# The last keys' products of an attention step put between its whole-chunk scores and its whole-chunk attn @ v

## The chip, the cores and the metric

The kernel runs on one core of one Trainium2 chip. The metric is the device time of one execution in microseconds. A core has TensorE (matmuls, PE in the profile; its loads of weights are PEld), VectorE (DVE), ScalarE (ACT), GpSimd (POOL) and SyncE (SP, which here only issues DMAs). Matmuls write to PSUM, and VectorE and ScalarE read it from there.

## What is computed

```python
def _attn_ref(q, k, v):                      # each (8, 12, 448, 64): batch, heads, sequence, width of a head
    scale = 1.0 / np.sqrt(q.shape[-1])
    scores = scale * np.matmul(q, k.transpose(0, 1, 3, 2)) - np.log(S)
    attn = 1.0 / (1.0 + np.exp(-scores))     # sigmoid, no softmax
    return np.matmul(attn, v)

def reference(q, k, v, w_in, w_out, s, b):
    x = attn_out.transpose(0, 2, 1, 3).reshape(B * S, H * D)   # 3584 x 768
    h = np.maximum(x @ w_in, 0.0)            # 3584 x 2048
    return (s * (h * h) + b) @ w_out         # 3584 x 768
```

## The kernel before

Attention comes first, in 24 steps (n = 0 to 23), and the feed-forward part fills the rest of the time. A step takes one batch and a quad of four heads: two pairs i = 0, 1, each with two heads j on the halves of the 128 partitions. The scores are computed with keys on the partitions. The 448 keys of a head are three whole chunks of 128 keys (c = 0, 1, 2) and 64 last keys. So a step has six tiles of whole-chunk scores (i, c), each for two heads, and one tile for the last keys of all four heads.

TensorE does four things in a step, each with its own shape of matmul. A shape such as 64\*128 in the profile says how many rows and columns of the array one matmul takes.

- `scores` (line 413, 64\*128): the six whole-chunk tiles. From step 1 on each is made of three products, since q and k are split into a high and a low part (qkh, qkl); 36 matmuls. Step 0 has single products of unsplit data (line 419).
- `attn_v` (line 445, 128\*64): the six tiles of sigmoids times v, 24 matmuls (12 pairs) that add up in the PSUM tile pav.
- `scores_last` (line 434, 64\*64): the last keys' scores, psc_l, 8 matmuls in two groups of four, for step n + 1. Step 0 does its own as well.
- `attn_v_last` (line 454, 64\*64): the last keys' sigmoids times v, 8 matmuls in two groups of four that also add into pav.

ScalarE turns each tile of scores into a tile of sigmoids (`sigmoid`, line 394), in the order (0,0), (0,1), (0,2), (1,0), (1,1), (1,2); then it makes the high part of the next step's q and k, does some jobs on weights (line 208, 258 and others), and takes the last-keys sigmoid a_l for the next step. VectorE makes the low part, converts weights, and copies pav out (`store_x`, line 461).

The order on each engine is that of the code, since the schedule is manual. PSUM is what ties the engines to each other. The pool ps_qk has three buffers with the tag psc, which are taken in turn:

```python
pl, tag = (ps_av, "pav") if (i, c) == (0, 2) else (ps_qk, "psc")
o = psc[i, c] = pl.tile([P, 2, 512], F32, tag=tag, name=f"psc_{b}_{t}_{i}_{c}")
...
psc = ps_qk.tile([P, 2, 512], F32, tag="psc", name=f"psc_{b}_{t}_l")
```

So chunk (0, 2) is computed in the one buffer of ps_av, which then becomes pav, and the other five and the last keys' tile go through the three buffers of ps_qk. From step 1 on TensorE takes them in the order (0,0), (0,1), (1,0), (0,2), (1,1), (1,2). A tile that takes a used buffer waits until the sigmoid that read the old one has ended.

Of the kernel before, what the change touches and what calls it, by code (L numbers as in the profile page):

```python
# [11 lines left out]
F32 = mybir.dt.float32  # L12
# [82 lines left out]
def sigmoid_attention_relu2_ffn(  # L95
# [11 lines left out]
    B, NQ, P, _, _, S = qk.shape  # L107
    D = v.shape[5]
    NF, _, DM = w_in.shape
# [13 lines left out]
    def pool(stack, name, bufs, side=None, space=None):  # L123
        kw = dict(side=side) if side else {}
        if space is not None:
            kw["space"] = space
        return stack.enter_context(
            tc.tile_pool(name=name, bufs=bufs, reuse_waits="tile", **kw)
        )
# [22 lines left out]
    first = ExitStack()  # L152
# [201 lines left out]
    ps_av = pool(at, "ps_av", 1, space=PSUM, side="right")  # L354
# [5 lines left out]
    def load(b, t, first=False):  # L360
        x = ld.tile([P, 2, 2, S], F32, tag="qk", name=f"qk_{b}_{t}")
        if first:
            nc.sync.dma_start(x[:, 0, 1, :P], qk[b, t][:, 0, 1, :P])
            nc.scalar.dma_start(x[:, 0, 0], qk[b, t][:, 0, 0])
            nc.sync.dma_start(x[:, 0, 1, P:], qk[b, t][:, 0, 1, P:])
            nc.scalar.dma_start(x[:, 1, 0], qk[b, t][:, 1, 0])
            nc.sync.dma_start(x[:, 1, 1], qk[b, t][:, 1, 1])
        else:
            nc.sync.dma_start(x, qk[b, t])
        return [x]  # L370

    def load_v(b, t, ld_):
        vt = ldv.tile([P, 7, 2, D], F32, tag="v", name=f"v_{b}_{t}")
        nc.sync.dma_start(vt, v[b, t])
        ld_.append(vt)
# [6 lines left out]
    def parts_hi(b, t, ld_):  # L382

        hi, lo = (hl.tile([P, 2, NX], F32R, tag=h, name=f"qk{h}_{b}_{t}") for h in "hl")
        nc.scalar.copy(hi, flat(ld_[0]))
        ld_.append((hi, lo))

    def parts_lo(ld_):
        hi, lo = ld_[-1]
        sub(lo, flat(ld_[0]), f32(hi))  # L390
# [6 lines left out]
    def scores(b, t, ld_):  # L397
        x = ld_[0]
        two = ld_.pop() if len(ld_) > 2 else None
        a = {}  # L400
        psc = {}
        order = [(i, c) for i in range(2) for c in range(3)]
        if two:
            order[2:4] = order[3], order[2]
        for i, c in order:

            pl, tag = (ps_av, "pav") if (i, c) == (0, 2) else (ps_qk, "psc")
            o = psc[i, c] = pl.tile([P, 2, 512], F32, tag=tag, name=f"psc_{b}_{t}_{i}_{c}")
            if two:
                cols = slice(S + c * P, S + (c + 1) * P)  # L410
                for m, (wi, xi) in enumerate(PARTS):
                    for j, r in enumerate(half):
                        nc.tensor.matmul(  # L413
                            o[:, j, :S], two[wi][r, i, cols], two[xi][r, i, :S],
                            start=m == 0, stop=m == 2,
                        )
            else:
                for j, r in enumerate(half):
                    nc.tensor.matmul(  # L419
                        o[:, j, :S], x[r, i, 1, c * P : (c + 1) * P], x[r, i, 0, :],  # L420
                        start=True, stop=True,
                    )
            if two and i + c == 1 and i:
                continue
            for k in [(i, c)] + [(1, 0)] * (two is not None and (i, c) == (0, 2)):
                a[k] = sigmoid(psc[k], f"{b}_{t}_{k[0]}_{k[1]}")
        return a

    def scores_last(b, t, ld_):
        x = ld_[0]  # L430
        psc = ps_qk.tile([P, 2, 512], F32, tag="psc", name=f"psc_{b}_{t}_l")
        for j, r in enumerate(half):
            for i in range(2):
                nc.tensor.matmul(  # L434
                    psc[half[i], j, :S], x[r, i, 1, 3 * P :], x[r, i, 0, :],
                    start=True, stop=True,
                )
        return sigmoid(psc, f"{b}_{t}_l")

    def attn_v(b, t, ld_, a):  # L440
        pav = ps_av.tile([P, 2, 512], F32, tag="pav", name=f"pav_{b}_{t}")
        for i in range(2):
            for c in range(3):
                for j, r in enumerate(half):
                    nc.tensor.matmul(  # L445
                        pav[r, i, :S], ld_[1][:, 3 * i + c, j, :], a[i, c][:, j, :],
                        start=c == 0, stop=False,
                    )
        return pav

    def attn_v_last(ld_, a, pav):
        for i in range(2):
            for j, r in enumerate(half):
                nc.tensor.matmul(  # L454
                    pav[r, i, :S], ld_[1][half[i], 6, j, :], a[half[i], j, :],
                    start=False, stop=True,
                )

    def store_x(b, t, pav):
        o = xo.tile([P, 2, S], F32, tag="xo", name=f"xo_{b}_{t}")  # L460
        nc.vector.tensor_copy(o, pav[:, :, :S])
        nc.sync.dma_start(x_dram[b][:, 2 * t : 2 * t + 2], o)

    loaded = {0: load(*quads[0], first=True)}
# [18 lines left out]
    def ticks(n, part):  # L483
        for _, _, fn in sorted(plan.pop((n, part), ()), key=lambda x: x[:2]):
            fn()
# [98 lines left out]
    for n, (b, t) in enumerate(quads):  # L584
        ticks(n, "DVE")
        a = scores(b, t, loaded[n])
        if n == 0:
            al = scores_last(b, t, loaded[0])
        if n + 1 in TWO:
            parts_hi(*quads[n + 1], loaded[n + 1])  # L590
        ticks(n, "ACT")
        if n + 2 < NL:
            loaded[n + 2] = load(*quads[n + 2])
        ticks(n, "SP")
        for fn in stores:
            fn()
        stores.clear()
        if n == NL - 1:
            qkx.close()
            ps_h = pool(blk_ps, "ps_h", 2, space=PSUM)  # L600
        pav = attn_v(b, t, loaded[n], a)
        last = al
        if n + 1 < NL:
            al = scores_last(*quads[n + 1], loaded[n + 1])
        attn_v_last(loaded[n], last, pav)
        if n + 1 in TWO:
            parts_lo(loaded[n + 1])
        ticks(n, "END")
        store_x(b, t, pav)
        if n + 2 < NL:  # L610
            load_v(*quads[n + 2], loaded[n + 2])
# [142 lines left out]
    start = [(0, 0), (2, 0), (2, 1), (2, 2), (0, 2), (0, 1), (1, 1), (1, 2), (1, 0)]  # L754
# [175 lines left out]
    for n, blocks in enumerate(threes):  # L930
# [128 lines left out]
        for u, (i, p) in enumerate(L1):  # L1059
# [10 lines left out]
            for j in range(2):  # L1070
                m = 0
                for c in range(KC):
                    for wi, xi in PARTS:
                        nc.tensor.matmul(  # L1074
                            bk[:, j], wt[:, j, wi, c * P : (c + 1) * P], opd[i][xi][:, c, :],
                            start=i == ch[0] and m == 0,
                            stop=m == 3 * KC - 1,
# [111 lines left out]
        for j, (i, p) in enumerate(L2):  # L1189
# [8 lines left out]
            for e, tk in LAST if end else [(e, slice(TB)) for e in range(KC)]:  # L1198
# [3 lines left out]
                for f in range(2):  # L1202
                    for m, (wi, gi) in enumerate(PARTS):
                        nc.tensor.matmul(  # L1204
                            o, wt[:, f, wi, e * P : (e + 1) * P], g[gi][:, f, tk],
                            start=(end or i == ch[0] and p == 0) and f == 0 and m == 0,
                            stop=p == NPP - 1 and f == 1 and m == 2,
# [61 lines left out]
```

## Time and profile before

| | |
|---|---|
| median of 3 runs | 1039.59 us (1039.41 to 1039.64) |
| profiled execution | 1039.4 us, its span in the trace 1037.5 us |
| TensorE busy | 1033.5 us (100%) |
| VectorE, ScalarE busy | 832.7 us (80%), 618.3 us (60%) |
| granted TensorE clock | 1.000 of full speed |
| 16 DMA engines | 277 GB/s on the mean |

The span runs from the first to the last instruction that the trace shows; the time of the same execution is 1.9 us longer. A share is a mean over the attention steps and the feed-forward part, which have different limits. The end of a matmul is modelled in the trace, so a start tells more than an end. A weight load (PEld) has a row of its own beside the matmul that uses it.

### The profile page before, as it was taken

What the parts mean: (1) busy time and instruction counts of PE and PEld (TensorE: products, weight loads), DVE (VectorE), ACT (ScalarE), POOL (GpSimd) and SP (SyncE); (2) the same over time, 40 slices, a digit from 0 to 9 for tenths busy, and PEclk for the clock granted to TensorE, in tenths of its full rate; (3) what the DMA queues carried; (4) which work ended last, traced back from release to release, by engine and by line L of the source; (5) the groups of instructions that cost most, each with busy time, mean ns of one, the idle gap of its engine ahead of it and who ended that gap; (6) DMA issues with size and microseconds to landing.
All of it is one profiled execution on the core that took longest, in us unless ns stands there. A gap on an engine that the chain in (4) does not pass through costs nothing.

```text
span 1037.5 us, 13890 instructions
## 1 busy us (share of the span) xinstructions
PE 1033.5 (100%) x5287; PEld 780.6 (75%) x5287; DVE 832.7 (80%) x900; ACT 618.3 (60%) x667; POOL 0.2 (0%) x4
## 2 busy tenths in 40 slices
PE   9999999999999999999999999999999999999998
PEld 4545555555888888888888888888888888888887
DVE  4999999995988965898898897796455789888777
ACT  7999999988776755574445344344445335552432
POOL 0000000000000000000000000000000000000000
PEclk9999999999999999999999999999999999999999
DMA  8788989995999999999686676897666666676763
GB/s 325 273 333 337 354 325 395 344 397 193 333 364 367 357 408 410 342 342 320 201 269 190 217 229 220 290 318 249 197 192 194 194 193 195 192 228 217 221 228 118
DMA packets 101569, 287.16 MB, mean 277 GB/s; under 512 B 10241, under 2 KB 20353, under 8 KB 101505
## 3 DMA queue, kind: packets, MB, share of 16 engines
q1 hardware_dynamic: 101216, 285.84, 79.2%
q8 instruction: 42, 0.69, 0.3%
q10 hardware_dynamic: 288, 0.46, 0.1%
q14 instruction: 23, 0.18, 0.0%
HBM read 198.18 MB, written 88.08 MB: 276 GB/s over the span
## 4 chain that ended last, share of the span: by engine, by line
PE 100%; DVE 0%; issue 0%
PE o L1204 31%; PE h L1074 31%; PE pav L445 11%; PE psc L413 9%; PE ph L553 6%; PE po L744 6%; PE psc_l L434 2%; PE pav L454 2%; PE psc L419 1%; PE idle L472 0%; DVE C_t L183 0%; DVE zero L165 0%; DVE nls L166 0%
## 5 line engine op out<-in xcount | busy, mean ns | idle before, releaser
L1074 PE MATMUL h<-s_1h,wu 128*128 128x512 f32 x480 | 148.0, 389 | 0.0
L1074 PE MATMUL h<-s_0h,wu 128*128 128x512 f32 x480 | 147.8, 389 | 0.0
L394 ACT ACTIVATE a<-psc,nls 128x896 f32<-128x896 f32 x144 | 132.7, 1009 | 12.9 <-PE psc L413 10.2
L445 PE MATMUL pav<-a,v 128*64 128x448 f32 x576 | 113.5, 543 | 0.0
L1074 PEld LDWEIGHTS h<-s_1h,wu 128*128 128x128 f32 x480 | 90.1, 188 | 18.8
L1074 PEld LDWEIGHTS h<-s_0h,wu 128*128 128x128 f32 x480 | 90.1, 188 | 18.6
L947 ACT COPY G<-h 128x1024 f32<-128x1024 f32 x48 | 48.9, 1018 | 85.0 <-PE h L1074 58.0
L839 ACT ACTIVATE G<-G,b_sb,s_sb 128x1024 f32<-128x1024 f32 x48 | 59.8, 1245 | 61.4 <-DVE G L836 60.7
L1074 PE MATMUL h<-s_0l,wu 128*128 128x512 f32 x240 | 93.4, 389 | 0.0
L1074 PE MATMUL h<-s_1l,wu 128*128 128x512 f32 x240 | 93.4, 389 | 0.0
L445 PEld LDWEIGHTS pav<-a,v 128*64 128x64 f32 x576 | 39.2, 137 | 64.0 <-issue 44.8
L180 DVE TENSOR_TENSOR G<-G,h 128x1024 f32<-128x1024 f32 x40 | 48.7, 1219 | 39.0 <-PE h L1074 38.9
L1204 PE MATMUL o<-g_3h,wu 128*128 128x512 f32 (+1 forms) x244 | 79.0, 385 | 0.0
L1204 PE MATMUL o<-g_0h,wu 128*128 128x512 f32 x240 | 78.8, 389 | 0.0
L1204 PE MATMUL o<-g_1h,wu 128*128 128x512 f32 x240 | 78.8, 389 | 0.0
L1204 PE MATMUL o<-g_2h,wu 128*128 128x512 f32 x240 | 78.8, 389 | 0.0
L744 PE MATMUL po<-g,w 128*128 128x512 f32 x288 | 67.7, 389 | 0.0
L744 PEld LDWEIGHTS po<-g,w 128*128 128x128 f32 x288 | 54.1, 188 | 11.2
L553 PE MATMUL ph<-x0h,w 128*128 128x512 f32 x192 | 61.7, 390 | 0.0
L413 PE MATMUL psc<-qkh 64*128 64x448 f32 x276 | 53.0, 380 | 0.0
L1204 PEld LDWEIGHTS o<-g_3h,wu 128*128 128x128 f32 x244 | 45.7, 188 | 9.3
L1074 PEld LDWEIGHTS h<-s_0l,wu 128*128 128x128 f32 x240 | 45.0, 188 | 9.4
(152 smaller groups left out, 2025.4 us busy)
## 6 DMA issues: line engine op xcount, KB each, us to landing
wu<-wd SPq DMA_DIRECT2D x240, 512.0 KB, 4.3
wd<-t SPq DMA_DIRECT2D x36, 768.0 KB, 8.0
qk<-qk_t SPq DMA_DIRECT2D x23, 896.0 KB, 7.2
st<-w_out SPq DMA_DIRECT2D x16, 768.0 KB, 9.3
st<-w_in SPq DMA_DIRECT2D x16, 768.0 KB, 9.5
wd<-w SPq DMA_DIRECT2D x16, 768.0 KB, 5.8
v<-v_t SPq DMA_DIRECT2D x24, 448.0 KB, 5.6
xd<-xo SPq DMA_DIRECT2D x24, 448.0 KB, 4.3
```

What stands on the lines that cost most here:

```text
L180: nc.vector.tensor_tensor(o, x, y, op=ALU.add)
L394: nc.scalar.activation(a, psc[:, :, :S], AF.Sigmoid, bias=nls, scale=SCALE)
L413: nc.tensor.matmul(o[:, j, :S], two[wi][r, i, cols], two[xi][r, i, :S], start=m == 0, stop=m == 2,)
L434: nc.tensor.matmul(psc[half[i], j, :S], x[r, i, 1, 3 * P :], x[r, i, 0, :], start=True, stop=True,)
L445: nc.tensor.matmul(pav[r, i, :S], ld_[1][:, 3 * i + c, j, :], a[i, c][:, j, :], start=c == 0, stop=False,)
L454: nc.tensor.matmul(pav[r, i, :S], ld_[1][half[i], 6, j, :], a[half[i], j, :], start=False, stop=True,)
L553: nc.tensor.matmul(ph, w[:, k, wi, kc * P : (kc + 1) * P], x0[h][xi][:, cc, :], start=m == 0, stop=m == 3 * NCC - 1,)
L744: nc.tensor.matmul(pos[e], w[:, k, wi, kc * P : (kc + 1) * P], g[:, gi, :], start=first and i == 0, stop=last and i == 2,)
L839: nc.scalar.activation(x, x, AF.Identity, bias=b_sb, scale=s_sb)
L947: nc.scalar.copy(g(m, h), bk)
L1074: nc.tensor.matmul(bk[:, j], wt[:, j, wi, c * P : (c + 1) * P], opd[i][xi][:, c, :], start=i == ch[0] and m == 0, stop=m == 3 * KC - 1, sk ...
L1204: nc.tensor.matmul(o, wt[:, f, wi, e * P : (e + 1) * P], g[gi][:, f, tk], start=(end or i == ch[0] and p == 0) and f == 0 and m == 0, stop ...
```

## The change

In the loop over the steps, `attn_v_last` of step n and `scores_last` of step n + 1 now come directly behind the whole-chunk scores of step n, in this order, and the whole-chunk `attn_v` comes behind them. Before, it was `attn_v`, `scores_last`, `attn_v_last`. The matmul that clears pav (`start=True`) is now that of the last keys, and the one that closes it that of the whole chunks. Step 0 keeps whole chunks first, and its `scores_last` for step 1 comes behind `attn_v_last`. In step 23 there is no next step, so only the two products with v change places.

```diff
-    def attn_v(b, t, ld_, a):
-        pav = ps_av.tile([P, 2, 512], F32, tag="pav", name=f"pav_{b}_{t}")
+    def attn_v(ld_, a, pav, first):
...
-                        start=c == 0, stop=False,
+                        start=first and c == 0, stop=first is False and c == 2,
...
-    def attn_v_last(ld_, a, pav):
+    def attn_v_last(ld_, a, pav, first):
...
-                    start=False, stop=True,
+                    start=first, stop=not first,
...
-        pav = attn_v(b, t, loaded[n], a)
-        last = al
+        pav = ps_av.tile([P, 2, 512], F32, tag="pav", name=f"pav_{b}_{t}")
+        if n == 0:
+            attn_v(loaded[n], a, pav, True)
+        attn_v_last(loaded[n], al, pav, n > 0)
         if n + 1 < NL:
             al = scores_last(*quads[n + 1], loaded[n + 1])
-        attn_v_last(loaded[n], last, pav)
+        if n > 0:
+            attn_v(loaded[n], a, pav, False)
```

TensorE's instructions in step 1, before, from the first whole-chunk product with v to the last-keys scores of step 2 (names end in b_t_i_c and the buffer's number, l stands for the last keys; in brackets the engines or DMA queues whose semaphore the instruction waits for; an instruction here is two matmuls in the trace). The last-keys attn @ v (line 454), without a wait, and then step 2's scores come behind these:

```order
L445 MATMUL pav_1_337<-a_1_0_0_282,v_1_186 64x448 [waits DMAHW1_49,Activation_49]
L445 MATMUL pav_1_337<-a_1_0_0_282,v_1_186 64x448
L445 MATMUL pav_1_337<-a_1_0_1_291,v_1_186 64x448 x2
L445 MATMUL pav_1_337<-a_1_0_2_307,v_1_186 64x448 x2
L445 MATMUL pav_1_337<-a_1_1_0_309,v_1_186 64x448 [waits Activation_49]
L445 MATMUL pav_1_337<-a_1_1_0_309,v_1_186 64x448
L445 MATMUL pav_1_337<-a_1_1_1_318,v_1_186 64x448 [waits Activation_49]
L445 MATMUL pav_1_337<-a_1_1_1_318,v_1_186 64x448
L445 MATMUL pav_1_337<-a_1_1_2_327,v_1_186 64x448 [waits Activation_49]
L445 MATMUL pav_1_337<-a_1_1_2_327,v_1_186 64x448
L434 MATMUL psc_2_l<-qk_2_234 64x448 [waits DMAHW4_49]
L434 MATMUL psc_2_l<-qk_2_234 64x448 x3
```

The same place in the changed kernel, from the end of step 1's whole-chunk scores on, where line 452 is `attn_v_last` and line 444 is `attn_v`; step 2's scores come behind these:

```order
L413 MATMUL psc_1_1_2_320<-qkh_1_229,qkl_1_230 128x448 x2
L452 MATMUL pav_1_337<-a_1_l,v_1_186 64x448 [waits DMAHW1_49,Activation_49]
L452 MATMUL pav_1_337<-a_1_l,v_1_186 64x448 x3
L434 MATMUL psc_2_l<-qk_2_234 64x448 [waits DMAHW4_49,Activation_49]
L434 MATMUL psc_2_l<-qk_2_234 64x448 x3
L444 MATMUL pav_1_337<-a_1_0_0_282,v_1_186 64x448 x2
L444 MATMUL pav_1_337<-a_1_0_1_291,v_1_186 64x448 x2
L444 MATMUL pav_1_337<-a_1_0_2_307,v_1_186 64x448 x2
L444 MATMUL pav_1_337<-a_1_1_0_309,v_1_186 64x448 x2
L444 MATMUL pav_1_337<-a_1_1_1_318,v_1_186 64x448 [waits Activation_49]
L444 MATMUL pav_1_337<-a_1_1_1_318,v_1_186 64x448
L444 MATMUL pav_1_337<-a_1_1_2_327,v_1_186 64x448 [waits Activation_49]
```

The products of lines 454 and 434 moved ahead of the whole chunks and changed places with each other. The last-keys scores (psc_2_l) waited for a DMA alone and now wait for ScalarE as well; the same bracket stands at each of the 22 last-keys scores issued in steps 1 to 22. The wait for v's DMA and for ScalarE that stood at the first whole-chunk product of pav now stands at the first last-keys product. The wait for ScalarE at the whole chunk (1, 0) is gone; those at (1, 1) and (1, 2) stay.

In step 0 TensorE had this behind the last pair of whole chunks (the last sigmoid's product with v is the pair for chunk (1, 2)):

```order
L445 MATMUL pav_0_238<-a_0_1_2_220,v_0_164 64x448 [waits Activation_49]
L445 MATMUL pav_0_238<-a_0_1_2_220,v_0_164 64x448
L434 MATMUL psc_1_l<-qk_1_162 64x448 [waits DMAHW5_49,PE_49]
L434 MATMUL psc_1_l<-qk_1_162 64x448 x3
L454 MATMUL pav_0_238<-a_0_l,v_0_164 64x448 [waits Activation_49]
L454 MATMUL pav_0_238<-a_0_l,v_0_164 64x448 x3
L413 MATMUL psc_1_0_0_275<-qkh_1_229 128x448 [waits PE_49,Activation_49]
```

Here the changed kernel has:

```order
L444 MATMUL pav_0_238<-a_0_1_2_220,v_0_164 64x448 [waits Activation_49]
L444 MATMUL pav_0_238<-a_0_1_2_220,v_0_164 64x448
L452 MATMUL pav_0_238<-a_0_l,v_0_164 64x448 [waits Activation_49]
L452 MATMUL pav_0_238<-a_0_l,v_0_164 64x448 x3
L434 MATMUL psc_1_l<-qk_1_162 64x448 [waits DMAHW5_49,PE_49]
L434 MATMUL psc_1_l<-qk_1_162 64x448 x3
L413 MATMUL psc_1_0_0_275<-qkh_1_229 128x448 [waits PE_49,Activation_49]
```

The last-keys scores for step 1 (psc_1_l) and the last-keys attn @ v of step 0 changed places, with the same waits as before. On ScalarE, VectorE and SyncE the order of the instructions is the same in both kernels.

## Rows read from the trace of the kernel before

**Rows 1.** Page: engine table (busy us, share, instructions); chain that ended last.
```profile
PE 1033.5 (100%) x5287; PEld 780.6 (75%) x5287; DVE 832.7 (80%) x900; ACT 618.3 (60%) x667; POOL 0.2 (0%) x4
...
PE 100%; DVE 0%; issue 0%
```

**Rows 2.** Timeline, TensorE: start, length, line, tiles; beginnings of steps 2, 11 and 23.
```profile
27.07 0.47 PE L413 MATMUL psc<-qkh 64*128 64x448 f32 x2
...
118.87 0.47 PE L413 MATMUL psc<-qkh 64*128 64x448 f32 x2
...
241.33 0.47 PE L413 MATMUL psc<-qkh 64*128 64x448 f32 x2
```

**Rows 3.** Timeline, TensorE, step 11 from its last scores on; runs of one shape.
```profile
122.43 0.36 PE L413 MATMUL psc<-qkh,qkl 64*128 64x448 f32 x2
122.74 0.97 PE L445 MATMUL pav<-a,v 128*64 128x448 f32 x4
...
126.93 0.55 PE L445 MATMUL pav<-a,v 128*64 128x448 f32 x2
127.40 0.98 PE L434 MATMUL psc_l<-qk 64*64 64x448 f32 x8
128.21 0.93 PE L454 MATMUL pav<-a_l,v 64*64 64x448 f32 x8
129.07 0.47 PE L413 MATMUL psc<-qkh 64*128 64x448 f32 x2
```

**Rows 4.** Timeline, ScalarE, step 11: third and fourth sigmoid of its scores.
```profile
121.68 1.01 ACT L394 ACTIVATE a<-psc,nls 128x896 f32<-128x896 f32 x1
...
122.59 1.00 ACT L394 ACTIVATE a<-psc,nls 128x896 f32<-128x896 f32 x1
```

**Rows 5.** Timeline, step 0: fourth sigmoid (ACT), first four last-keys scores (PE).
```profile
8.53 1.02 ACT L394 ACTIVATE a<-psc,nls 128x896 f32<-128x896 f32 x1
...
9.60 0.61 PE L434 MATMUL psc_l<-qk 64*64 64x448 f32 x4
```

**Rows 6.** Step 10: a weight load (PEld), its matmuls; all matmuls of line 434.
```profile
117.64 0.15 PEld L454 LDWEIGHTS pav<-a_l,v 64*64 64x64 f32 x4 [0.22 <-issue]
...
118.01 0.93 PE L454 MATMUL pav<-a_l,v 64*64 64x448 f32 x8
...
L434 PE MATMUL psc_l<-qk x192: 536/562/588, 9.6 to 240.1; 64*64 64x448 f32 x192
```

**Rows 7.** Timeline, step 7: last-keys sigmoid, weight load of chunk (1,0), matmuls.
```profile
78.22 1.00 ACT L394 ACTIVATE a_l<-psc_l,nls 128x896 f32<-128x896 f32 x1
...
79.28 0.19 PEld L413 LDWEIGHTS psc<-qkh 64*128 64x128 f32 x2
...
79.15 0.37 PE L413 MATMUL psc<-qkh,qkl 64*128 64x448 f32 x2
79.35 0.40 PE L413 MATMUL psc<-qkh 64*128 64x448 f32 x2
79.59 0.36 PE L413 MATMUL psc<-qkl,qkh 64*128 64x448 f32 x2
```

**Rows 8.** Timeline, TensorE: beginnings of steps 7 and 8.
```profile
78.03 0.47 PE L413 MATMUL psc<-qkh 64*128 64x448 f32 x2
...
88.30 0.47 PE L413 MATMUL psc<-qkh 64*128 64x448 f32 x2
```

**Rows 9.** Timeline, ScalarE: last-keys sigmoid for step 1, first sigmoid of step 1.
```profile
16.22 1.01 ACT L394 ACTIVATE a_l<-psc_l,nls 128x896 f32<-128x896 f32 x1 [0.85 <-PE psc_l L434]
...
17.82 1.01 ACT L394 ACTIVATE a<-psc,nls 128x896 f32<-128x896 f32 x1 [0.59 <-PE psc L413]
```

**Rows 10.** DMA of q and k: issue for step 23, its landing, all landings.
```profile
L369 SPq DMA_DIRECT2D qk<-qk_t x1: 427/427/427, 228.2 to 228.2; - x1
...
DMA to landing us min/median/max: 7.2/7.2/7.2
...
DMA to landing us min/median/max: 2.6/6.9/10.9
```

More of the change, by code (lines that the diff above doesn't have):

```diff
@@ L446, in attn_v @@
                         pav[r, i, :S], ld_[1][:, 3 * i + c, j, :], a[i, c][:, j, :],
-                        start=c == 0, stop=False,
+                        start=first and c == 0, stop=first is False and c == 2,
                     )
-        return pav
-    def attn_v_last(ld_, a, pav):
+    def attn_v_last(ld_, a, pav, first):
         for i in range(2):
```

## The prediction

> **What bounds the kernel now.** I read the page's engine table first, then its chain of waits, then the timeline of TensorE step by step, and beside it the timelines of ScalarE and of the weight loads. The table has TensorE busy for 1033.5 of 1037.5 us, and the chain that ended last is 100% TensorE [rows 1]. So the kernel is one row of matmuls, and a change of order can only move the time by opening or closing gaps in that row. Ends of matmuls are modelled in the trace, so I read gaps from starts.
>
> The change lies in the attention phase: 24 steps, of which steps 1 to 22 have the same shape. Step 2 begins at 27.07, step 11 at 118.87, step 23 at 241.33 [rows 2], which makes (241.33 - 27.07) / 21 = 10.20 us a step. Step 11 is one of the even ones [rows 3]: the last pair of whole-chunk scores starts at 122.43, attn @ v at 122.74, the next step's last-keys scores at 127.40, the last-keys attn @ v at 128.21, and step 12 at 129.07. Within one shape of matmul the starts follow at a steady pace (0.20 for a pair of scores; 0.37 to 0.38 for a pair of attn @ v or for four of the last keys' products). At each change of shape the next start comes later than that pace: 0.31 instead of 0.20 at 122.74, 0.47 instead of 0.38 from the last pair of attn @ v (126.93) to 127.40, and 0.86 instead of 0.75 from 128.21 to 129.07.
>
> One of these gaps has a second cause. Attn @ v writes into the PSUM tile pav, which held the scores of chunk (0, 2) until the third sigmoid of the step had read them. That sigmoid starts at 121.68, takes 1.01 and ends at 122.69 [rows 4], and attn @ v starts 0.05 behind it. So ScalarE, 0.91 us a sigmoid, walks just in front of TensorE here. It is the fact that decides the forecast.
>
> **The change part by part.** Nothing is added or removed: the 24 + 8 + 8 matmuls of a step stay, on VectorE and SyncE every job keeps its place, and ScalarE's order stays too. Three things could change.
>
> *Changes of shape.* A step has three before (scores to attn @ v, attn @ v to last keys, last keys to scores) and three after (scores to last keys, last keys to attn @ v, attn @ v to scores), since the two last-keys products stay next to each other. Each kind that the trace has costs the same: a start about 0.09 late and a first load of weights that is not hidden, 0.05 for 64 columns. The sum takes 0.
>
> *The tile pav.* Last-keys attn @ v is now the first to write pav, so it inherits the wait on the third sigmoid: it starts where attn @ v does now, 122.74 in step 11. Cost 0. The last write of pav still comes at the step's end, so VectorE's copy of it and the store behind it stay.
>
> *The slot of the last-keys scores.* The pool of score tiles has three buffers. Six tiles a step pass through it in turn, (0,0), (0,1), (1,0), (1,1), (1,2), last keys, so the last-keys tile of step n + 1 takes the buffer of chunk (1, 0) of step n, whose sigmoid is the fourth. Before, that sigmoid was 3.8 us in the past when the product came (123.59 against 127.40). Now the product stands 0.8 us behind the third sigmoid, and the rows of the change show the new wait on ScalarE in each of steps 1 to 22. In step 11 the eight matmuls ahead of it would take 0.81, as last-keys scores do now (127.40 to 128.21), so it could start at 122.74 + 0.81 = 123.55. The fourth sigmoid starts at 122.59, takes 1.00 [rows 4], and with the 0.05 seen above releases it at 123.64. It is **0.09 late**. That such a slot wait binds can be seen in step 0, where scores and last keys already stand in this order: the fourth sigmoid ends at 8.53 + 1.02 = 9.55, and the last-keys scores start at 9.60 [rows 5].
>
> To this comes the load of weights. In a steady row the load runs one group ahead: the weights for the product that starts at 118.01 are loaded at 117.64 [rows 6]. A wait holds the load, and what it would have hidden then lies open. Step 7 shows it: the last-keys sigmoid there runs 78.22 to 79.22 [rows 7], the load for chunk (1, 0), which needs its buffer, starts only at 79.28 instead of about 79.15 (with the matmul ahead of it). The matmul shown at 79.35 keeps its place in the record, yet its successor comes after 0.24 instead of 0.20: 0.03 to 0.04 lost although the sigmoid ended 0.13 before the matmul was due. For 64 columns the open load is the 0.05 by which the first matmul after a change of shape is longer (587 against 536 ns) [rows 6]. So the step loses 0.09 + 0.05 = **0.14**. From below, this is 0.09 (load already done) or nothing; from above, a full restart such as at a change of shape would start the product 0.47 behind the last group, 123.55 - 0.375 + 0.47 = 123.64, the same instant. So I take 0.14.
>
> The Trainium skill (TensorE: Matmul & The Clock Gate, Part 3, "The mechanism") says that TensorE pulls weight loads ahead of matmuls in flight out of a window of 64. If that reached past a load that waits, the sum would be 22 x 0.09 = 2.0 us. The load at 79.28 speaks against it here: it stood held with its semaphore.
>
> *The sum.* 22 steps x 0.14 = 3.1 us. Step 7 is late now by 0.07 (78.03 to 88.30 is 10.27) [rows 8], because ScalarE came to its last-keys sigmoid late; a longer step 6 gives ScalarE 0.14 more, and that lateness goes; step 16 is the only other step late in this way: -0.15 together. In step 0 the last-keys scores for step 1 change places with a group of eight and come 0.80 later; their sigmoid, which now starts at 16.22 and had waited for them [rows 9], starts near 17.03 and pushes the first sigmoid of step 1 from 17.82 [rows 9] to 17.94, some +0.04 at the fourth. Together **+3.0 us**. Behind the attention phase TensorE is just as dense, so nothing gives it back. The profiled execution's 1039.4 becomes 1042.4; the median of the runs shown, 1039.59, lies 0.2 above it and becomes 1042.6. I say 1042.5.
>
> *What is needed earlier.* Last-keys scores of step n + 1 read that step's q and k 3.8 us sooner. The tightest transfer is the one for step 23, issued at 228.2 and landing 7.2 later, 235.4 [rows 10]. It would be read at about 241.33 - 10.20 + 4.77 + 0.14 = 236.0: 0.6 of room, cost 0. If it took as long as the longest of these, 10.9 [rows 10], TensorE would wait 3.0 there.
>
> **The rivals.**
> *The bare wait.* The load is done ahead and only 0.09 a step is lost: 22 x 0.09, less the corrections, is 1.9, time 1041.5. For it: in the record of step 7 the matmul start itself did not move. Against it: its successor did. This is the case of the page's rule above.
> *Late data.* The transfer for step 23 misses its 0.6: up to 3.0 on top, 1042.5 to 1045.6. For it: transfers of this kind scatter from 2.6 to 10.9. Against it: a schedule this regular repeats, and 7.2 was measured with the same neighbours.
> *Nothing happens.* The slot wait is hidden, because the eight matmuls ahead take 0.1 longer than I think: 1039.5. Against it: the same eight at 127.40 take 0.81.
> *The other side: a cheap change of shape.* Attn @ v to scores is the one kind that the trace does not have. If it were free, 0.09 plus the 0.11 by which the first pair of scores is longer would go, 0.20 x 22 = 4.4 us, against the 3.0 of the wait: 1038.1. It decides from 0.14 a step on. Against it: last keys to scores, attn @ v to last keys, and scores to attn @ v start alike late, whatever the two shapes are [rows 3].
>
> **How the numbers follow.** A measurement of this kernel tells about 0.2% (2.1 us) from no change: 1037.5 and 1041.7 are the bounds. Held load, 1042.0 to 1043.2: 0.62. Bare wait: 0.14. Late data or another new wait: 0.13. Nothing: 0.06. Cheap change of shape: 0.05, of which 0.03 would pass 0.2%. So slower 0.62 + 0.13 = 0.75, same 0.14 + 0.06 + 0.02 = 0.22, faster 0.03. The range 1041.0 to 1044.0 holds the first two cases and a third of the third, 0.80.
>
> **What would show it.** Steps of about 10.34 instead of 10.20 from 2 to 22. In each, last-keys attn @ v starts 0.05 behind the third sigmoid, the loads of the last-keys scores 0.05 behind the fourth, and the first group of these scores lasts as long as after a change of shape or starts that much later. Attn @ v waits for no sigmoid. From the start of step 23 on all is shifted by one constant. The prediction is wrong if the last-keys scores follow the group ahead of them without a gap, if the start of scores behind attn @ v comes at another distance than 0.47 behind the last pair, or if the transfer for step 23 is what they wait for.

## The result and the profile after

| | before | after |
|---|---|---|
| median | 1039.41 us (1039.18 to 1039.64, 5 runs) | 1043.26 us (1042.21 to 1043.69, 5 runs) |
| profiled execution, its span | 1039.4 us, 1037.5 us | 1042.94 us, 1040.6 us |

The change made the kernel slower: the ratio is 1.0036, with a 95% interval from 1.0025 to 1.0047. The runs of after lie 1.5 us apart, those of before 0.5 us. A few executions far above all others of the same kernel are left out here and in the experiments. The granted TensorE clock is 1.000 in both.

The page of after, its engine table and the chain that ended last, answers to [rows 1]:

```profile
PE 1035.8 (100%) x5287; PEld 778.2 (75%) x5287; DVE 832.4 (80%) x900; ACT 617.7 (59%) x667; POOL 0.2 (0%) x4
...
PE 98%; DMA 1%; DVE 1%; SPq 0%; issue 0%
```

TensorE is as dense as before, and the count of instructions is the same. New in the chain is a DMA with 1% of the span, which the chain's table by line names as that of q and k. This is how long the transfer took, and not what it cost.

The beginnings of steps 2, 11, 22 and 23 on TensorE answer to [rows 2]:

```profile
27.16 0.47 PE L413 MATMUL psc<-qkh 64*128 64x448 f32 x2
...
120.14 0.47 PE L413 MATMUL psc<-qkh 64*128 64x448 f32 x2
...
233.88 0.47 PE L413 MATMUL psc<-qkh 64*128 64x448 f32 x2
...
244.46 0.47 PE L413 MATMUL psc<-qkh 64*128 64x448 f32 x2
```

Step 2 begins 0.09 later than before and step 23 3.13 later. The span grew by 3.1, so the whole loss lies in the attention steps and almost all of it in steps 2 to 22. Steps 2 to 21 take (233.88 - 27.16) / 20 = 10.34 us each, where the mean before was 10.20. Step 22 alone takes 10.58.

TensorE in step 11, from the last-keys attn @ v to the beginning of step 12, answers to [rows 3]:

```profile
124.01 0.98 PE L452 MATMUL pav<-a_l,v 64*64 64x448 f32 x8
124.91 0.98 PE L434 MATMUL psc_l<-qk 64*64 64x448 f32 x8
125.82 4.73 PE L444 MATMUL pav<-a,v 128*64 128x448 f32 x24
...
130.00 0.55 PE L444 MATMUL pav<-a,v 128*64 128x448 f32 x2
130.48 0.47 PE L413 MATMUL psc<-qkh 64*128 64x448 f32 x2
```

The third and fourth sigmoid of this step on ScalarE answer to [rows 4]:

```profile
122.94 1.01 ACT L394 ACTIVATE a<-psc,nls 128x896 f32<-128x896 f32 x1
...
123.85 1.00 ACT L394 ACTIVATE a<-psc,nls 128x896 f32<-128x896 f32 x1
```

The weight loads of the two last-keys products, with what they waited for in brackets:

```profile
124.01 0.21 PEld L452 LDWEIGHTS pav<-a_l,v 64*64 64x64 f32 x8 [0.33 <-ACT a L394]
124.90 0.21 PEld L434 LDWEIGHTS psc_l<-qk 64*64 64x64 f32 x8 [0.69 <-ACT a L394]
```

The row at 130.00 is the last pair of those at 125.82. The third sigmoid ends at 123.95, and last-keys attn @ v starts 0.06 behind it, as attn @ v did before. The fourth ends at 124.85, and the last-keys scores load their weights at 124.90. They start 0.90 behind the group ahead of them, where two adjacent groups of this shape stood 0.81 apart [rows 3]: 0.09 late.

### The profile page after: what moved, and what is told of

It is laid out like the page before. It is cut to its first block, busy times and chain, and to the rows that moved or that the text cites. A ratio compares the mean times of both kernels' runs of the same rounds, so it can differ in the third digit from the quotient of the medians.

```text
span 1040.6 us, 13911 instructions
## 1 busy us (share of the span) xinstructions
PE 1035.8 (100%) x5287; PEld 778.2 (75%) x5287; DVE 832.4 (80%) x900; ACT 617.7 (59%) x667; POOL 0.2 (0%) x4
## 4 chain that ended last, share of the span: by engine, by line
PE 98%; DMA 1%; DVE 1%; SPq 0%; issue 0%
PE o L1205 31%; PE h L1075 31%; PE pav L444 10%; PE psc L413 8%; PE ph L551 6%; PE po L745 6%; PE pav L452 2%; PE psc_l L434 2%; DMA qk<-qk_t 1%; PE psc L419 0%; DVE wf L210 0%; DVE st L213 0%; DVE xo L459 0%; DVE st L217 0%; DVE wf L220 0%
## 5 line engine op out<-in xcount | busy, mean ns | idle before, releaser
L1075 PEld LDWEIGHTS h<-s_1l,wu 128*128 128x128 f32 x240 | 45.0, 188 | 9.4
```

The costliest lines, as they stand in the source:

```text
L1075: nc.tensor.matmul(bk[:, j], wt[:, j, wi, c * P : (c + 1) * P], opd[i][xi][:, c, :], start=i == ch[0] and m == 0, stop=m == 3 * KC - 1, sk ...
```

## The experiments

The kernels ran beside before on the same chips, where its medians were 1039.3 to 1039.5 us and its runs lay 1.2 to 1.5 us apart. A ratio is that to before on the same chip.

### e1: the wait taken away by a shorter sigmoid

In the changed kernel, with w = 224 for chunk (1, 0) from step 2 on:

```diff
+        nc.scalar.activation(a[:, :, :w], psc[:, :, :w], AF.Sigmoid, bias=nls, scale=SCALE)
...
-                        pav[r, i, :S], ld_[1][:, 3 * i + c, j, :], a[i, c][:, j, :],
+                        pav[r, i, :S], ld_[1][:, 3 * i + c, j, :], a[0 if c == 0 else i, c][:, j, :],
```

> The changed kernel, but from step 2 on the fourth sigmoid (chunk (1, 0)) takes 224 of 448 columns per head, so that the buffer of the last-keys scores comes free some 0.45 us sooner. The products of attn @ v for chunk (1, 0) read the sigmoids of chunk (0, 0) instead, in all steps; this part of the result is left out. Theory (the slot wait and the load that it holds are the whole loss): steps 2 to 22 go back to 10.19 us, last-keys scores follow the group ahead after 0.36 from last start to first start, span 1037.4 to 1037.9, time 1039.3 to 1039.9. Rival (the new changes of shape, or something else of the order, cost the time): steps stay at 10.33, time 1042 to 1043.5.

Measured: 1039.38 us (10 runs), ratio 1.0001 [0.9991, 1.0010]; span 1037.5. The loss is gone. The beginnings of steps 2 and 23 of this kernel, and in step 10 the fourth sigmoid, the weight loads and the matmuls of the last-keys scores:

```profile
27.62 0.47 PE L414 MATMUL psc<-qkh 64*128 64x448 f32 x2
...
241.32 0.47 PE L414 MATMUL psc<-qkh 64*128 64x448 f32 x2
...
112.72 0.65 ACT L395 ACTIVATE a<-psc,nls 128x448 f32<-128x448 f32 x1
...
113.42 0.44 PEld L436 LDWEIGHTS psc_l<-qk 64*64 64x64 f32 x8 [0.31 <-ACT a L395]
...
113.70 0.93 PE L436 MATMUL psc_l<-qk 64*64 64x448 f32 x8
```

The load is still held until 0.05 behind the sigmoid (113.37), but that is 0.28 ahead of its matmul. The eight matmuls start 0.80 behind the group ahead of them, and they span 0.93 and not 0.98, so the first load is hidden. Steps 2 to 22 take 213.70 us together (10.17 each, 10.26 in steps 7 and 16), against 214.26 in before and 217.30 in after. In this execution the transfer for step 23 came just in time too (step 22 takes 10.17), so the late data that e3 is about are absent as well.

### e2: the sigmoid only a little shorter

The same edit with w = 400.

> As the run with the short fourth sigmoid, but with 400 of 448 columns per head: the sigmoid gets about 0.10 us shorter, so its end frees the buffer just before the matmul would be due (0.80 behind the start of the group ahead) but after the load of its weights would be due (0.43). The same part of the result is left out. Theory (a wait holds the load, 0.05 of which then lies open): about 0.045 us a step remains, steps of 10.235, time 1040.2 to 1040.8. Rival (the bare wait counts, the load is done ahead): nothing remains, steps of 10.19, time 1039.3 to 1039.9.

Measured: 1040.47 us (9 runs), ratio 1.0010 [1.0001, 1.0019]; span 1038.6. Step 11:

```profile
123.02 0.94 ACT L395 ACTIVATE a<-psc,nls 128x800 f32<-128x800 f32 x1
...
124.01 0.21 PEld L436 LDWEIGHTS psc_l<-qk 64*64 64x64 f32 x8 [0.60 <-ACT a L395]
...
119.35 0.47 PE L414 MATMUL psc<-qkh 64*128 64x448 f32 x2
124.01 0.98 PE L436 MATMUL psc_l<-qk 64*64 64x448 f32 x8
129.58 0.47 PE L414 MATMUL psc<-qkh 64*128 64x448 f32 x2
```

Here the sigmoid ends at 123.96, and the matmuls start at 124.01, 0.81 behind the group ahead: they are not late at all. But the eight span 0.98 again, and the step takes 10.23, against 10.17 in e1 (most steps take 10.21 to 10.24). Steps 2 to 21 take 204.60 us, in e1 203.53, which is 0.05 a step. The shorter sigmoid of e1 gives no other lead: in most steps of both kernels the last-keys attn @ v starts 3.84 into the step. So the open load costs 0.05 by itself. Step 22 takes 10.55 here, since the transfer for step 23 landed late (see e3). The 0.05 is the part of the forecast that the rival "bare wait" left out. The rule that this rival rested on, in the Trainium skill (TensorE: Matmul & The Clock Gate, Part 3, "The mechanism"), is that TensorE pulls weight loads ahead of matmuls in flight; the trace agrees for a load without a wait (0.37 ahead [rows 6]) and for one whose semaphore comes early enough (0.28 ahead in e1), and it shows a load held as long as its semaphore is missing.

### e3: the load of q and k for step 23 issued earlier

In the changed kernel, at the start of a step and behind the jobs of ScalarE:

```diff
+        if n == 21:
+            loaded[n + 2] = load(*quads[n + 2])
...
-        if n + 2 < NL:
+        if n + 2 < NL and n != 21:
```

> The changed kernel, with the load of q and k for step 23 issued at the start of step 21, ahead of a store that waits 4.8 us for VectorE. Theory (in the changed kernel the last-keys scores for step 23 wait for this load, 0.25 us in the profiled execution and more in others, which is also why the runs scatter from 1042.2 to 1043.7): step 22 takes 10.33 instead of 10.58, the median falls to 1042.3 to 1042.7 and all runs lie within 0.5 us. Rival (the scatter has another cause): step 22 is shorter, but the runs still lie 1 to 1.5 us apart and the median stays near 1043.

Measured: 1042.48 us (1042.35 to 1042.64, 6 runs), ratio 1.0029 [1.0018, 1.0041]. The median is 0.8 lower than that of after, and the runs lie 0.3 us apart instead of 1.5. In after, the last-keys scores for step 23 waited for the transfer; the rows of TensorE in step 22, and issue and landing of the transfer, are

```profile
237.75 0.98 PE L452 MATMUL pav<-a_l,v 64*64 64x448 f32 x8
...
238.88 0.98 PE L434 MATMUL psc_l<-qk 64*64 64x448 f32 x8 [0.16 <-DMA qk<-qk_t]
...
L369 SPq DMA_DIRECT2D qk<-qk_t x1: 413/413/413, 230.8 to 230.8; - x1
...
DMA to landing us min/median/max: 8.0/8.0/8.0
```

and in e3 the same two are

```profile
238.67 0.98 PE L434 MATMUL psc_l<-qk 64*64 64x448 f32 x8
...
DMA to landing us min/median/max: 10.0/10.0/10.0
```

In after the data came at 230.8 + 8.0 = 238.8, and the matmuls started 238.88 - 237.75 = 1.13 behind the group ahead instead of 0.90. In e3 the transfer was issued at 227.2 and took even longer, 10.0, but landed at 237.2, 1.5 ahead of its use; step 22 takes 10.33 like the others. So the wait for late data and its removal are shown by the two traces. That all of the 0.8 in the median and all of the scatter come from it is not shown: the intervals of the two ratios overlap, and runs of before, whose trace has no such wait, lie 1.2 us apart beside e3. Other traces have the wait as well. In e2, e5 and e8 the transfer landed 7.9, 8.4 and 9.7 behind its issue, and the last-keys scores of step 22 came 0.32, 0.71 and 1.13 late.

### e5: the sigmoids of chunks (1, 0) and (1, 1) exchanged

In the changed kernel, which makes the order of the sigmoids (0,0), (0,1), (0,2), (1,1), (1,0), (1,2):

```diff
-            for k in [(i, c)] + [(1, 0)] * (two is not None and (i, c) == (0, 2)):
+            for k in [(i, c)] + [(1, 0)] * (two is not None and (i, c) == (1, 1)):
```

> The changed kernel, with the fourth and fifth sigmoid of each step exchanged ((1, 1) before (1, 0)), so that the buffer of the last-keys scores comes free one sigmoid later. Nothing is left out. Theory (these scores wait for the sigmoid of chunk (1, 0)): they start 0.89 us later in steps 1 to 22, steps of 11.22, 22 x 0.89 = 19.6 us on top, time 1062 to 1063.5. Rival (the loss has another cause, the slot wait is hidden): time as the changed kernel, 1042 to 1044.

Measured: 1042.91 us (4 runs), ratio 1.0031 [1.0017, 1.0046]: no change, a clear miss. Most steps take 10.34; step 22, with its late data, takes 11.04. The fourth sigmoid, now that of chunk (1, 1), and the load for the last-keys scores in step 10:

```profile
114.04 1.00 ACT L394 ACTIVATE a<-psc,nls 128x896 f32<-128x896 f32 x1
...
115.09 0.21 PEld L434 LDWEIGHTS psc_l<-qk 64*64 64x64 f32 x8 [0.69 <-ACT a L394]
```

The load still follows the fourth sigmoid (115.04) by 0.05. In the built program the last-keys tile now has the bank of (1, 1), where in after it has that of (1, 0). So the buffers are not simply taken in turn, as the text ahead of the prediction has it: both programs fit a rule by which a tile gets the buffer that is released first. The wait is for the fourth sigmoid, whichever chunk that is, and this experiment could not move it.

### e4 and e4b: the shorter sigmoid in the old order

This is the edit of e1 on the kernel before.

> Control: the kernel before, with the same shortened fourth sigmoid (224 of 448 columns per head from step 2 on) and the same products of chunk (1, 0) read from the sigmoids of chunk (0, 0). Theory: nothing in the old order waits for this sigmoid, so relief of ScalarE alone gives 0 to -0.2 us, time 1039.1 to 1039.6. Rival (less work on ScalarE is worth something whatever the order): 1 us or more faster, below 1038.4.

> The control with the short fourth sigmoid in the old order once more, for its profile. Expected from its times so far (0.6 us below the kernel before): steps of 10.165 instead of 10.193, because attn @ v no longer waits for the end of the third sigmoid and follows the scores after 0.29 instead of 0.31. If steps are 10.19 the gain lies elsewhere.

Measured: 1038.7 us (10 runs), ratio 0.9992 [0.9983, 1.0002], and 1038.8 us (7 runs), ratio 0.9994 [0.9983, 1.0005]. In e4b, the beginnings of steps 2 and 23, and beginning of step 11, attn @ v, beginning of step 12:

```profile
26.89 0.47 PE L414 MATMUL psc<-qkh 64*128 64x448 f32 x2
...
240.59 0.47 PE L414 MATMUL psc<-qkh 64*128 64x448 f32 x2
...
118.48 0.47 PE L414 MATMUL psc<-qkh 64*128 64x448 f32 x2
122.33 4.73 PE L447 MATMUL pav<-a,v 128*64 128x448 f32 x24
...
128.65 0.47 PE L414 MATMUL psc<-qkh 64*128 64x448 f32 x2
```

Attn @ v starts 3.85 into the step instead of 3.87 [rows 2, 3], and steps 2 to 22 take 213.70 us, the very sum of e1. So with a short fourth sigmoid these steps cost the same in the old and the new order: the order itself, with its three changes of shape, costs nothing there, and what is left between before and after is the wait for the fourth sigmoid and the late data of step 22. The whole execution of e1 is still 0.8 longer (spans 1037.5 and 1036.7). Of this, 0.19 lies in step 1, whose sigmoid isn't shortened and whose wait stays. Another 0.54 lies ahead of step 1, and its cause is open; the kernels before, e9 and e10, which are the same up to there, begin step 1 anywhere from 16.35 to 16.84. That the old order gains too, 0.03 a step, is because ScalarE is then earlier at the next steps' third sigmoid, for which attn @ v waits.

### e6: the two last-keys products exchanged, behind attn @ v

In the kernel before:

```diff
         pav = attn_v(b, t, loaded[n], a)
-        last = al
+        attn_v_last(loaded[n], al, pav)
         if n + 1 < NL:
             al = scores_last(*quads[n + 1], loaded[n + 1])
-        attn_v_last(loaded[n], last, pav)
```

> Half of the change: whole-chunk attn @ v stays directly behind the scores, and only the two last-keys products change places, attn @ v of the last keys before the last-keys scores. Theory: no slot wait, but the last-keys scores end 0.80 later, right at the end of the step; their sigmoid starts near 0.19 us of the next step, the first sigmoid of that step is pushed from 0.98 to 1.10, the third to 3.90, and attn @ v with it: 0.08 a step, 22 steps, +1.5 to +2.0 us, time 1041.0 to 1041.5. Rival (the order of these two is free): 1039.4.

Measured: 1039.90 us (10 runs), ratio 1.0005 [0.9995, 1.0015]; steps of 10.22. On ScalarE the last-keys sigmoid, on TensorE the beginning of step 11 and attn @ v:

```profile
118.66 1.01 ACT L394 ACTIVATE a_l<-psc_l,nls 128x896 f32<-128x896 f32 x1 [1.02 <-PE psc_l L434]
...
118.52 0.47 PE L413 MATMUL psc<-qkh 64*128 64x448 f32 x2
...
122.41 4.73 PE L445 MATMUL pav<-a,v 128*64 128x448 f32 x24
```

The last-keys sigmoid now waits for its scores and holds up the sigmoids behind it, so that attn @ v starts 3.89 into the step: 0.02 to 0.03 a step, where 0.08 was expected. The direction was right. The size was not, because the sigmoid comes 0.14 into the step and not 0.19: no change of shape stands ahead of its scores any more.

### e7: only the last keys' scores put back to the step's end

In the changed kernel:

```diff
         attn_v_last(loaded[n], al, pav, n > 0)
-        if n + 1 < NL:
-            al = scores_last(*quads[n + 1], loaded[n + 1])
         if n > 0:
             attn_v(loaded[n], a, pav, False)
+        if n + 1 < NL:
+            al = scores_last(*quads[n + 1], loaded[n + 1])
```

> The other half: last-keys attn @ v stands directly behind the scores, then whole-chunk attn @ v, and the last-keys scores stand at the end of the step. Four changes of shape a step instead of three, no slot wait. Theory: one more change of shape costs 0.09 + 0.05, and the late last-keys scores 0.08 as in the swap alone: 0.22 a step, +4.5 to +5.2 us, time 1044 to 1044.8. Rival (a change of shape costs nothing of its own): +1.5 to +2, time 1041 to 1041.5.

Measured: 1043.74 us (4 runs), ratio 1.0042 [1.0026, 1.0057]; steps of 10.38, 0.19 more than before instead of 0.22. TensorE from the beginning of step 11 on:

```profile
120.42 0.47 PE L413 MATMUL psc<-qkh 64*128 64x448 f32 x2
...
124.32 0.98 PE L452 MATMUL pav<-a_l,v 64*64 64x448 f32 x8
125.23 4.73 PE L444 MATMUL pav<-a,v 128*64 128x448 f32 x24
129.90 0.98 PE L434 MATMUL psc_l<-qk 64*64 64x448 f32 x8
130.81 0.47 PE L413 MATMUL psc<-qkh 64*128 64x448 f32 x2
```

The wait for the fourth sigmoid is gone from the last-keys scores, and the kernel is no faster for it, for the two groups of one shape no longer stand next to each other. Each of them now takes 0.91 to the start of the next group, where next to each other they took 0.81 and 0.86 [rows 3]; in e6, with last-keys attn @ v first as here, 0.80 and 0.86. So the fourth change of shape costs 0.16 a step (10.38 against the 10.22 of e6), of which 0.05 is the open first load. The Trainium skill (TensorEngine Tiling (Array Packing), "Key Properties") says that a change of tiling mode drains TensorE, without a price. The trace agrees that such a change costs time, 0.16 for these shapes; that TensorE is drained, no row here shows.

### e8, e9 and e10: the fourth sigmoid later

A copy on ScalarE ahead of the fourth sigmoid: e8 in the changed kernel, e9 in the kernel before, e10 in the kernel before with a[0, 2] in place of a[0, 0].

```diff
+                if two is not None and k == (1, 0):
+                    nc.scalar.copy(a[0, 0][:, :, :224], a[0, 0][:, :, :224])
```

> The changed kernel with one more job on ScalarE between the third and the fourth sigmoid of steps 1 to 23: a copy onto itself of 224 columns per head of the finished sigmoids (0, 0), about 0.5 us, so that the result stays the same and the fourth sigmoid ends that much later. The buffers of the score tiles stay as they were. Theory (the last-keys scores wait for the fourth sigmoid): they start 0.5 us later in each of the steps 1 to 22, steps of about 10.84, 11 us on top of the changed kernel, time 1053 to 1055. Rival (they wait for something else, or the wait has slack): time 1042 to 1044.

Measured: 1051.11 us (4 runs), ratio 1.0114 [1.0099, 1.0129]; steps of 10.74, but 11.87 in step 22 with its late data. The copy, the fourth sigmoid and the load for the last-keys scores in step 10:

```profile
116.94 0.55 ACT L427 COPY a<-a 128x448 f32<-128x448 f32 x1
117.39 1.01 ACT L394 ACTIVATE a<-psc,nls 128x896 f32<-128x896 f32 x1
...
118.46 0.21 PEld L436 LDWEIGHTS psc_l<-qk 64*64 64x64 f32 x8 [1.12 <-ACT a L394]
```

The load again follows the sigmoid (118.40) by about 0.05, and the whole delay goes into the step: 10.74 - 10.34 = 0.40. The mechanism was right; the size, 10.84, was too high by 0.1 because the copy takes 0.45 of ScalarE's time and not 0.5, and the third sigmoid starts 0.06 sooner in the step (2.74 instead of 2.80).

> Control: the kernel before with the same extra copy on ScalarE. Theory: in the old order nothing on TensorE waits closely for the fourth sigmoid, so most steps stay at 10.19; only the steps in which ScalarE has the most jobs come late to the last-keys sigmoid and start their first sigmoid late. ScalarE has about 9.6 us of work in a step of 10.2, so it is nearly full: +1 to +6 us, time 1040.5 to 1045.5, well below the same copy in the changed kernel. Rival (more work on ScalarE costs the same in any order): +11 us, 1050.

Measured: 1048.57 us (4 runs), ratio 1.0091 [1.0074, 1.0108]; steps of 10.60 to 10.64: missed. The copy in step 11, and the first loads of attn @ v:

```profile
126.22 0.55 ACT L427 COPY a<-a 128x448 f32<-128x448 f32 x1
...
126.83 0.20 PEld L447 LDWEIGHTS pav<-a,v 128*64 128x64 f32 x4 [0.70 <-ACT a L427]
```

The copy is written into the sigmoids of chunk (0, 0), which are the first that attn @ v reads in the old order. So the control had brought in a wait of its own. Therefore e10:

> The control of the copy again, with the flaw of the last one taken out: the kernel before with the same ScalarE copy (224 of the 448 columns of each head) between the third and the fourth sigmoid of steps 1 to 23, now in place on the sigmoids of chunk (0,2), which attn @ v reads third, and not of (0,0), which it reads first. The result is unchanged. The theory: in the old order no product at the head of the group waits for the fourth sigmoid, so moving it later by the copy's 0.41 us (the shift that the copy caused in the changed kernel) is mostly covered by the products of (0,0) and (0,1); steps of 10.19 to 10.3 us, 1039.3 to 1042 us. The rival: the old order waits for the fourth sigmoid, or for ScalarE as a whole, as much as the new one, and the steps come out near 10.6 us, 1048 to 1049 us, as with the copy on (0,0).

Measured: 1044.93 us (4 runs), ratio 1.0054 [1.0037, 1.0070]. Most steps take 10.35 to 10.40; five (7, 10, 14, 16 and 19) take 10.67 to 10.76, in step 10 because ScalarE's last-keys sigmoid starts only 0.66 into the step. That is more than the theory gave and half of the rival. A new wait has come in, seen in the loads at the start of step 11 and in the table of all waits (us in total, times, longest):

```profile
121.31 0.19 PEld L413 LDWEIGHTS psc<-qkl,qkh 64*128 64x128 f32 x2 [0.19 <-DVE qkl L183]
...
PEld psc L413 <- DVE qkl L183: 4.0, 22, 0.2
```

The last-keys scores don't wait for the fourth sigmoid here. But ScalarE comes later to the high part of the next step's q and k, VectorE to the low part, and the second product of each step waits for it: 4.0 us in all. So the control for the step's middle is only partly clean: it shows that in the old order the same delay costs 0.16 in an ordinary step, by another wait, against 0.40 in the new one.

## Why the prediction was right

**The bound.** TensorE's row of matmuls sets the end in both kernels, and nothing gave the loss back: the 3.13 by which step 23 is late is the growth of the span.

**Changes of shape, cost 0.** Right. From the last pair of attn @ v to the scores a start comes 0.48 behind (130.00 to 130.48), as from attn @ v to the last keys before (0.47 [rows 3]), so the rival "cheap change of shape" is out. Better evidence is that steps 2 to 22 take the same 213.70 us in e1 and e4b. The price of one change, which has no part in the sum, was set a little low: 0.09 + 0.05, where e7 gives 0.11 + 0.05.

**The tile pav, cost 0.** Right: last-keys attn @ v starts 3.87 into the step, where attn @ v started before. Whole-chunk attn @ v waits for no sigmoid from step 1 on.

**The slot of the last-keys scores, 0.14 a step.** Right in both parts: 0.09 of late start in after, and 0.05 of open load, which e2 shows by itself. Taking the wait away takes the loss away (e1), and moving the sigmoid by some 0.4 moves the step by 0.40 (e8). In after's table of waits the loads of the last-keys scores stand with 23 waits (step 0 has one of them), and the longest matmul of line 434 is again the 587 ns of an open first load:

```profile
L434 PE MATMUL psc_l<-qk x192: 536/536/587, 9.6 to 239.3; 64*64 64x448 f32 x192
...
PEld psc_l L434 <- ACT a L394: 15.9, 23, 0.9
```

The total of such waits is time in which the loads stood idle, most of which lies under running matmuls, so it is no measure of the loss. What the prediction had wrong here is the reason for the buffer: it isn't taken in turn (e5). The result is the same in this order of sigmoids.

**Steps 7 and 16, -0.15.** Right in the cause, too small in size. Steps 7 and 8 of after begin at

```profile
78.82 0.47 PE L413 MATMUL psc<-qkh 64*128 64x448 f32 x2
...
89.16 0.47 PE L413 MATMUL psc<-qkh 64*128 64x448 f32 x2
```

which is 10.34, like most others, where it had been 10.27 against 10.20 [rows 8]. Before, step 16 was late by 0.10 (10.29), and step 17, which the prediction overlooked, by 0.04 (10.24). All three are even in after, which gives back 0.22 and not 0.15.

**Step 1, +0.04 beyond the 0.14.** Too much. Its last-keys and first sigmoid are

```profile
16.93 1.01 ACT L394 ACTIVATE a_l<-psc_l,nls 128x896 f32<-128x896 f32 x1 [1.46 <-PE psc_l L434]
17.84 1.00 ACT L394 ACTIVATE a<-psc,nls 128x896 f32<-128x896 f32 x1
```

so the first sigmoid comes 0.02 later than before [rows 9], not 0.12. I had moved the last-keys sigmoid by 0.80 and forgotten that its scores lose the change of shape ahead of them, which is 0.05; another 0.04 is that step 1 began sooner (16.80, before 16.84). Step 1 takes 10.37, 0.14 more than before, and step 2 begins 0.09 late instead of 0.18.

**The sum.** For steps 2 to 21 it gave 20 x 0.14 - 0.15 = 2.65. Measured: 206.72 (233.88 - 27.16) against 204.07 before (27.07 to the beginning of step 22 at 231.14), which is 2.65. That both come to the same last digit is luck: the late steps gave back 0.22, and steps 12 and 18 of after take 10.37, 0.04 more than the others, for which no wait in the trace accounts. The span too comes out near the forecast (3.1 against 3.0) in part because two errors go opposite ways: step 2 began 0.09 sooner than forecast, and the next term cost 0.25.

**"What is needed earlier", cost 0.** This term was mis-sized. The transfer for step 23 landed 8.0 behind its issue and not 7.2 [rows 10], its room of 0.6 was gone, and step 22 lost 10.58 - 10.33 = 0.25 more in the profiled execution. The rival "late data" is thus true besides the held load, and not instead of it. The median is 0.8 above the 1042.5 that I said; with the transfer issued earlier (e3) it is 1042.48. How much of the 0.8 is this transfer stays open: 0.25 is shown, in the profiled execution. There is also a part of the time that the span does not hold. In the profiled execution the time grew by 3.5 and the span by 3.1, since the two were 1.9 apart before and are 2.3 apart after; they lie 1.9 to 2.5 apart in the runs of before, so this part is scatter that the forecast could not know. The argument that failed is "7.2 was measured with the same neighbours": one profiled execution gives one value (7.2 before, 7.4 in e1, 7.9 to 9.7 in after, e2, e5 and e8), and where a transfer has no slack its scatter comes into the time.

## What to carry to other kernels

Before moving a product ahead, list the buffers that it writes and the place of their last readers in the new order: a slot wait with 3.8 us of slack leaves no row in the trace of before, and the same wait with none decided this case. A wait costs the late start and the first weight load that it uncovers, and a matmul that is exactly on time can still pay the second. A moved product also eats the slack of its transfers: compare the room with the scatter of such transfers, not with one landing time.

## What was not expected of the hardware and the program

- A weight load that waits for a semaphore isn't pulled ahead, although its matmul starts on time (e2): 0.05 us for 64 columns. With the semaphore there earlier, the load ran 0.28 us ahead of its matmul (e1).
- From the end of a sigmoid to the load that waits for it 0.05 us pass, in each of after, e1, e2, e5 and e8.
- The old order was not free of ScalarE either: its attn @ v waits for the third sigmoid, and a shorter fourth one saves 0.03 us a step there (e4b).
- The transfer for step 23 took 7.2 us in before, 8.0 in after and 10.0 in e3. Issued 3.6 us sooner into the queue, it landed only 1.6 us sooner.
- An exchange of two readers of the pool's buffers exchanged the banks of the tiles too (e5). That the buffers go out in the order of their release fits both programs; it was not tried further.
